# Another order for the end of a gated-attention MoE kernel: its flag is read earlier, its last branch is turned round and hinted at the head of the program

## The chip, the cores and the metric

The kernel runs on one core of a Trainium2 chip. A core has five engines that run their own instruction streams: PE (TensorE, matrix products), DVE (VectorE), ACT (ScalarE), POOL (GpSimd) and SP (SyncE, which here only starts DMA transfers). They meet at semaphores. What is measured is the device time of one launch in microseconds (us); the median of three runs of the kernel before is 1458.15 us (1458.13 to 1458.2).

## The reference

```python
def _attn_ref(q, k, v, f_logit):            # (4, 8, 768, 48) each
    f = 1.0 / (1.0 + np.exp(-f_logit))
    for t in range(S):
        state = f[:, :, t, :, None] * state + np.einsum('bhd,bhe->bhde', k[:, :, t], v[:, :, t])
        y[:, :, t] = np.einsum('bhd,bhde->bhe', q[:, :, t], state)

def _moe_ref(x, w_gate, w1, w2):            # x: (3072, 384), 8 experts, hidden width 1024
    P = np.exp(logits - logits.max())       # logits = x @ w_gate
    for _ in range(8):
        P /= P.sum(1, keepdims=True) + 1e-09
        P /= P.sum(0, keepdims=True) + 1e-09
        P *= N / E
    for e in range(E):
        out += P[:, e:e + 1] * (np.maximum(x @ w1[e], 0.0) @ w2[e])
```

The output of the attention, transposed, is the x of the MoE.

## The kernel before, in words

All products are made in half precision with every operand split into a high and a low part, three matmuls to a product. After the attention and the gate come the experts. Experts 0 and 1 are done early and densely. For experts 2 to 7 the work is cut into 48 periods (expert, half of the hidden width, batch), and each period has a first and a second half. The first half makes 15 products into PSUM banks named A to F and combines them (a scheme that saves products, after Strassen); a table of events (EVENTS, L69) says which engine adds, moves, converts what. It leaves tiles in SBUF: kh, kl, and the sums kr, kf with their high parts kgh (made on ACT, L1425) and low parts kgl (made on POOL, L1428). The second half is three blocks (`paired`, L1217; t = 0, 1, 2), seven products each into two PSUM tiles called kyps and kxps; ACT moves a partial sum back into PSUM (`move`, L1251), DVE adds the finished quarter into the accumulator acc (`add`, L1254), and for some blocks POOL adds a staged tile (L1301, L1275). In the last period of a batch the accumulator is stored to the output (`store`, L1266).

In the running part the blocks of one period are interleaved with the products of the next. At the end nothing is left to interleave, and a hand-written table, CLOSING (L87), says in which order the last events of period 47 and the five blocks that are left run. A number in it advances one of these blocks by one step (0 and 1 are blocks 1 and 2 of period 46; 2, 3 and 4 are blocks 0, 1 and 2 of period 47), a tuple is an event, and 'v' is a step of the computation of the flag. ENDX says which PSUM bank each of these blocks takes. `pin` and `mm` tie the instructions of each engine into the order in which the table writes them.

The flag: the kernel's gate uses a fast way that is right only for values within bounds; a test over the whole run ends as one integer, `flag`, made by five tiny DVE operations (tile gd_r, L919 to L924) and two transposes on PE. At the end each of the five engines loads it into a register (L271) and branches on it (L272): where it is set, `general`, a slow version of the whole computation, is run. The code of `general` stands right behind the fast path, the end of the program behind that, so in a normal run each engine jumps over `general`. At 'hint' in CLOSING a hint for that branch is given to DVE, ACT and SP; it names the block "general" as the likely target.

Of the kernel before, what the change touches and what calls it, by code (L numbers as in the profile page):

```python
# [8 lines left out]
F32 = mybir.dt.float32  # L9
# [73 lines left out]
READDAT = (9, 14)  # L83
CHECKAT = (1, 5)
MAXAT = (2, 6)
ENDX = (('x', None), ('k0', None), ('x', 'B'), ('k2', None))
CLOSING = (('add', 'C', '+', 3), ('gd', 1, 'P'), ('gh', 0, 1), 0, 1, 0, ('hh', 'D', 2), 0, ('gl', 0, 0), ('gl', 0, 1), 1,  # L87
# [5 lines left out]
BY_VECTOR = ((0, 0), (1, 0), (2, 0), (2, 1))  # L93
ORDER = [(e, m, b) for e in range(2, NE) for m in range(2) for b in range(B)]
PAIRED = (0, 1, 2)
BY_POOL = (1,)
# [169 lines left out]
def tile_gla_moe(tc, qkf, vc, vt, wg, w1, w2, out):  # L266
    nc = tc.nc
    with tc.tile_pool(name="fl", bufs=1) as fp:
        flag = fp.tile([1, 1], I32, name="flag")
        fast(tc, qkf, vc, wg, w1, w2, out, flag)  # L270
        bad = nc.values_load(flag, min_val=0, max_val=1)  # L271
        with tc.If(bad > 0, label="general"):  # L272
            general(tc, qkf, vt, wg, w1, w2, out)


# [1 line left out]
def fast(ctx, tc, qkf, vc, wg, w1, w2, out, flag):  # L277
# [615 lines left out]
    def verdict():  # L893
# [12 lines left out]
        pin(nc.vector.tensor_scalar(out=g[:, 0:2], in0=g[:, 0:2], scalar1=-1.0, scalar2=None, op0=ALU.mult))  # L906
        pin(nc.vector.tensor_scalar(out=g[:, 2:3], in0=g[:, 2:3], scalar1=-BALANCE, scalar2=None, op0=ALU.mult))
        yield
        ps = pk.tile([128, 128], F32, name="gd_t", tag="D")
        mm(transpose=True, out=ps[0:7, :], in_=g, identity=identf)  # L910
        yield
        col = cst.tile([7, 1], F32, name="gd_c")
        pin(nc.vector.tensor_reduce(out=col, in_=ps[0:7, :], axis=AX.X, op=ALU.max))
        yield
        ps = pk.tile([128, 128], F32, name="gd_s", tag="k1")
        mm(transpose=True, out=ps[0:1, 0:7], in_=col, identity=identf[0:7, 0:7])
        yield
        r = cst.tile([1, 9], F32, name="gd_r")
# [295 lines left out]
    first = {b: min(n for n, p in enumerate(ORDER) if p[2] == b) for b in range(B)}  # L1214
    final = {b: max(n for n, p in enumerate(ORDER) if p[2] == b) for b in range(B)}

    def paired(n, h, t, tag="x", own=None):  # L1217
        e, m, b = ORDER[n]
        new = n == first[b]
        if new and t == PAIRED[0]:  # L1220
            acc[b] = accp.tile([128, 2, TT, DM], F32, name=f"acc{b}", tag="acc")
        p = (pk if own else psm).tile([128, DM], F32, name=f"kyps_{n}_{t}", tag=own or "m")
        q = pk.tile([128, DM], F32, name=f"kxps_{n}_{t}", tag=tag)
        x0, y0, x1 = q[:, 0:DH], p[:, 0:DH], p[:, DH:DM]
        p2 = lp.tile([128, DH], F32, name=f"part_{n}_{t}", tag="part", bufs=2)
        by_pool = t in BY_POOL and n < len(ORDER) - 1 and not new
        xx, yy = (acc[b][:, v, t, :].rearrange("p (s d) -> p s d", s=2) for v in range(2))
        direct = n == len(ORDER) - 1
        if not new and not direct:
# [33 lines left out]

        def store(v, half):
            r0, ds = (2 * b + v) * HS + t * 128, slice(0, DM) if half is None else slice(half * DH, half * DH + DH)
            (nc.scalar if direct and v else nc.sync).dma_start(out=out[r0:r0 + 128, ds], in_=acc[b][:, v, t, ds])  # L1266

        product(y0, None, (0, 0), start=True)
        product(x1, (None, 0), (None, 0))
        yield  # L1270
        move(x0, y0)
        move(p2, x1, scale=scale(1))
        if direct:
            for i in range(2):
                pin(nc.gpsimd.tensor_tensor(out=yy[:, i, :], in0=yy[:, i, :], in1=p2, op=ALU.add))  # L1275
        yield
# [6 lines left out]
        yield  # L1283
        product(x1, (None, 1), (None, 1))
        yield
        out_x(0, x0)
        add(yy[:, 1, :], x1, scale(1), yy[:, 1, :] if direct else p2)
        halved = direct and t == PAIRED[-1]
        if halved:
            for v in range(2):  # L1290
                store(v, v)
        yield
# [5 lines left out]
        for v, z, there in ((0, xx, not by_pool), (1, yy, new or direct)):  # L1298
            if not there:
                y = acc[b][:, v, t, :]  # L1300
                pin(nc.gpsimd.tensor_tensor(out=y, in0=y, in1=z.rearrange("p s d -> p (s d)"), op=ALU.add))  # L1301
            if n == final[b]:
                store(v, 1 - v if halved else None)

    def readds():
        todo = {b: [(o, v, t) for t in range(TT) for v in range(2) for o in range(2) if (o, 2 * b + v) in RAW] for b in range(B)}
# [62 lines left out]
    def event(ctxt, ev):  # L1369
# [39 lines left out]
        elif kind == 'ga':  # L1409
            hs['a', ev[2]] = [lp.tile([128, 2, 128], F16, name=f"ka{q}_{tag}_{ev[2]}", tag=f"ka{q}{ev[2]}", bufs=1) for q in "hl"]  # L1410
            pin(nc.scalar.activation(out=hs['a', ev[2]][0], in_=bk[:, :, 0:128], func=AF.Relu))
        elif kind == 'gf':
            ah, al = hs['a', ev[2]]
            pin(nc.vector.scalar_tensor_tensor(out=al, in0=bk[:, :, 0:128], scalar=0.0, in1=ah, op0=ALU.max, op1=ALU.subtract))
        elif kind == 'gb':
            ah, al = hs['a', ev[1]]
            pin((nc.gpsimd if ev[2] == 'P' else nc.vector).tensor_tensor(out=al, in0=hs['r', ev[1]][:, 0], in1=ah, op=ALU.subtract))
        elif kind == 'gh':
            _, t, i = ev
            if not i:  # L1420
                if t == 2:
                    hs['g', t] = [[hp.tile([128, 2, 2, 128], F16, name=f"kg{q}{i}_{tag}_{t}", tag=f"k{q}1{0}{i}", bufs=1) for i in range(2)] for q in "hl"]
                else:
                    hs['g', t] = [[lp.tile([128, 2, 2, 128], F16, name=f"kg{q}{i}_{tag}_{t}", tag=f"kg{q}{t}{i}", bufs=1) for i in range(2)] for q in "hl"]
            pin(nc.scalar.activation(out=hs['g', t][0][i], in_=hs['f' if i else 'r', t], func=AF.Copy))  # L1425
        elif kind == 'gl':
            _, t, i = ev
            pin((nc.vector if tag == str(PERIODS - 1) and (t, i) in BY_VECTOR else nc.gpsimd).tensor_tensor(out=hs['g', t][1][i], in0=hs['f' if i else 'r', t], in1=hs['g', t][0][i], op=ALU.subtract))  # L1428
        elif kind == 'hh':
            pin(nc.scalar.activation(out=hs['h', ev[2]][0], in_=bk, func=AF.Relu))  # L1430
        else:
            hh, hl = hs['h', ev[2]]
            pin(nc.vector.scalar_tensor_tensor(out=hl, in0=bk, scalar=0.0, in1=hh, op0=ALU.max, op1=ALU.subtract))
# [56 lines left out]
        raise RuntimeError("an event was left")  # L1490

    def close(what):
        if what == 'v':
            next(judged, None)
        elif isinstance(what, tuple):
            event(ctxt, what)
        else:
            next(going[what], None)

    hint = CLOSING.index('hint')  # L1500
    for what in CLOSING[:hint]:
        close(what)
    with tc.block():
        tc.mark_branch_hint_location("general", "LikelyTaken", [mybir.EngineType.DVE, mybir.EngineType.Activation, mybir.EngineType.SP])
        for what in CLOSING[hint + 1:]:
            close(what)
    if any(next(block, going) is not going for block in going):
        raise RuntimeError("a block was left")
    for _ in judged:
# [2 lines left out]
        raise RuntimeError("an early output was not added")  # L1512
    for _ in chained((checks, maxima, judged)):
        raise RuntimeError("a check was left")


def _layout(q, k, v, f_logit, wg, w1, w2):
# [38 lines left out]
```

## Time and profile before

| what | value |
|---|---|
| median of three runs | 1458.15 us |
| the profiled execution's own time | 1458.26 us |
| its span, from the first to the last instruction | 1456.4 us |
| granted TensorE clock, mean | 0.999 of full speed |
| busy in the span: PE, DVE, ACT, POOL | 1438.7, 1232.9, 1061.1, 1045.1 us |

The span is what the trace covers; 1.86 us of the profiled execution lie around it. Times below are counted from the start of the span. PE's matmuls overlap, each row shows its start and its length, and the next starts before it ends. An engine's name with a q (SPq, PEldq) stands for its sequencer, which runs loads of registers, branches, waits on semaphores and starts of DMA transfers; these are not counted as busy.

### The profile page before, as it was taken

How to read it: one execution, taken by the hardware profiler on the slowest of the kernel's cores; microseconds unless marked ns; L12 is line 12 of the kernel's file. 1: busy time of each engine (PE TensorE's matmuls, PEld its weight loads, DVE VectorE, ACT ScalarE, POOL GpSimd, SP SyncE). 2: the span in 40 equal slices, each digit the busy share in tenths (PEclk: the TensorE clock that was granted, in tenths of full speed). 3: DMA queues.
4: the chain of work that ended last, by engine and by line, in shares of the span. 5: the costliest groups of instructions: out<-in, count | busy, mean ns of one | idle time of the engine just before them, and what ended most of it. 6: DMA issues, size and time to landing. Idle time of an engine off the chain costs nothing.

```text
span 1456.4 us, 40359 instructions
## 1 busy us (share of the span) xinstructions
PE 1438.7 (99%) x16054; PEld 1256.4 (86%) x16054; DVE 1232.9 (85%) x2512; ACT 1061.1 (73%) x2382; POOL 1045.1 (72%) x1227
## 2 busy tenths in 40 slices
PE   8999999999999999999999999999999999999997
PEld 5888876666666899999999999999999999999997
DVE  8888788885787899888899999888889888888876
ACT  7766666663354877888888888888877787778764
POOL 4344434446429576999999999999988888888764
PEclk9999999999999999999999999999999999999999
DMA  9455455541011101122212111111111110000012
GB/s 282 122 136 128 117 133 129 118 117 32 29 33 38 35 23 35 51 57 62 61 56 61 51 50 49 46 45 51 50 34 34 34 34 23 17 18 13 2 53 82
DMA packets 105271, 92.58 MB, mean 64 GB/s; under 512 B 72080, under 2 KB 91920, under 8 KB 105072
## 3 DMA queue, kind: packets, MB, share of 16 engines
q1 hardware_dynamic: 104496, 89.32, 22.7%
q8 instruction: 127, 2.08, 0.6%
q14 instruction: 72, 0.59, 0.1%
q10 hardware_dynamic: 576, 0.59, 0.1%
HBM read 64.03 MB, written 14.16 MB: 54 GB/s over the span
## 4 chain that ended last, share of the span: by engine, by line


## 5 line engine op out<-in xcount | busy, mean ns | idle before, releaser
L305 PEld LDWEIGHTS <-k1h 128*128 128x128 f16 x2880 | 270.9, 98 | 21.5 <-issue 2.9
L305 PE MATMUL kyps<-k2h,kgh 128*128 128x192 f16 x1152 | 283.4, 246 | 0.2 <-ACT part L1251 0.2
L305 PE MATMUL kyps<-k2l,kgh 128*128 128x192 f16 x1152 | 283.4, 246 | 0.0
L305 PE MATMUL kyps<-k2h,kgl 128*128 128x192 f16 x1152 | 283.4, 246 | 0.0
L305 PEld LDWEIGHTS <-kgh 128*128 128x128 f16 x2304 | 212.0, 98 | 6.7 <-issue 0.4
L1428 POOL TENSOR_TENSOR kgl<-kf,kgh 128x512 f16<-128x512 f32 x143 | 190.4, 1331 | 1.5 <-ACT kgh L1425 1.5
L1428 POOL TENSOR_TENSOR kgl<-kr,kgh 128x512 f16<-128x512 f32 x141 | 175.1, 1242 | 10.8 <-ACT kgh L1425 10.6
L1254 DVE SCALAR_TENSOR_TENSOR yy<-kyps,pes,part 128x192 f32<-128x192 f32 x258 | 106.7, 414 | 88.5 <-PE kyps L305 78.1
L1301 POOL TENSOR_TENSOR acc<-acc,yy 128x384 f32<-128x384 f32 x129 | 129.5, 1004 | 57.4 <-DVE yy L1254 57.4
L305 PEld LDWEIGHTS <-k1l 128*128 128x128 f16 x1440 | 140.9, 98 | 16.3
L305 PE MATMUL yps<-w2h,hl 128*128 128x384 f16 x384 | 125.1, 326 | 0.5 <-DVE hl L477 0.5
L305 PE MATMUL yps<-w2h,hh 128*128 128x384 f16 x384 | 125.1, 326 | 0.1
L305 PE MATMUL yps<-w2l,hh 128*128 128x384 f16 x384 | 125.1, 326 | 0.0
L305 PEld LDWEIGHTS <-w1h 128*128 128x128 f16 x1344 | 96.9, 98 | 32.0 <-ACT w1h L373 0.4
L305 PEld LDWEIGHTS <-kh 128*128 128x128 f16 x1152 | 108.2, 98 | 7.0 <-issue 0.6
L305 PEld LDWEIGHTS <-kgl 128*128 128x128 f16 x1152 | 112.7, 98 | 0.2 <-issue 0.2
L305 PEld LDWEIGHTS <-hh 128*128 128x128 f16 x768 | 73.6, 98 | 44.2 <-issue 0.5
L1251 ACT ACTIVATE kyps<-kyps 128x192 f32<-128x192 f32 x144 | 45.7, 317 | 80.0 <-PE kyps L305 78.5
L1425 ACT ACTIVATE kgh<-kf 128x512 f16<-128x512 f32 x144 | 91.8, 638 | 0.5 <-DVE kf L1402 0.5
L1425 ACT ACTIVATE kgh<-kr 128x512 f16<-128x512 f32 x144 | 91.6, 636 | 0.0
L1379 ACT ACTIVATE cp<-kb_A 128x512 f32<-128x512 f32 x144 | 86.3, 599 | 2.7 <-DVE kb_A L1381 2.0
L1405 POOL TENSOR_TENSOR kr<-kr 128x256 f32<-128x256 f32 x96 | 72.4, 754 | 17.3 <-PE kb_C L305 8.7
(306 smaller groups left out, 5248.0 us busy)
## 6 DMA issues: line engine op xcount, KB each, us to landing
q<-in_qkf_dram SPq DMA_DIRECT2D x23, 672.0 KB, 5.4
k1r<-in_w_dram SPq DMA_DIRECT2D x24, 384.0 KB, 3.1
ys<-yr SPq DMA_DIRECT2D x48, 192.0 KB, 2.1
k2r<-in_w_dram SPq DMA_DIRECT2D x24, 384.0 KB, 3.1
yb<-ys SPq DMA_DIRECT2D x48, 192.0 KB, 2.4
vr<-in_vc_dram SPq DMA_DIRECT2D x24, 192.0 KB, 4.9
out_dram<-acc SPq DMA_DIRECT2D x20, 192.0 KB, 1.9
w1r<-in_w_dram SPq DMA_DIRECT2D x8, 384.0 KB, 9.4
```

Source lines behind the costliest of these rows:

```text
L305: ins = (nc.tensor.transpose if transpose else nc.tensor.matmul)(**kw)
L1251: pin(nc.scalar.activation(out=out, in_=in_, func=AF.Copy, **kw))
L1254: pin(nc.vector.scalar_tensor_tensor(out=y, in0=ps, scalar=p, in1=z, op0=ALU.mult, op1=ALU.add))
L1301: pin(nc.gpsimd.tensor_tensor(out=y, in0=y, in1=z.rearrange("p s d -> p (s d)"), op=ALU.add))
L1379: pin(nc.scalar.activation(out=fresh(ev[2]), in_=bk, func=AF.Copy))
L1405: pin((nc.gpsimd if ev[2] == 'P' else nc.vector).tensor_tensor(out=r[:, 0], in0=r[:, 1], in1=r[:, 0], op=ALU.subtract))
L1425: pin(nc.scalar.activation(out=hs['g', t][0][i], in_=hs['f' if i else 'r', t], func=AF.Copy))
L1428: pin((nc.vector if tag == str(PERIODS - 1) and (t, i) in BY_VECTOR else nc.gpsimd).tensor_tensor(out=hs['g', t][1][i], in0=hs['f' if i el ...
```

## The change

The table CLOSING and the table of banks are written anew, with the flag's steps early and a new entry 'load'. There the load of the flag into a register is put on each engine, in the order of the table (on PE behind the last matmul). The low parts kgl of the last period, four of which were made on DVE (BY_VECTOR), are all made on POOL. Block 1 of period 46 has its x sums added by DVE and not by ACT and POOL. The last block has a PSUM tile of its own (kzps) for x1. In all 144 blocks the add that frees x1 is issued ahead of the one that reads x0. Every store of the last period is cut into two halves of 96 KB, eight on SP and four on ACT; before there were, for these, 192 KB stores and some halves. The branch now reads "where the flag is clear go to `settled`", which is the end of the program; `general` is the block it falls into otherwise. The hint names `settled` and is given to DVE, ACT and PE ahead of the first instruction of the fast path.

```diff
@@ -267,9 +266,11 @@
         flag = fp.tile([1, 1], I32, name="flag")
-        fast(tc, qkf, vc, wg, w1, w2, out, flag)
-        bad = nc.values_load(flag, min_val=0, max_val=1)
-        with tc.If(bad > 0, label="general"):
+        tc.mark_branch_hint_location("settled", "LikelyTaken", [mybir.EngineType.DVE, mybir.EngineType.Activation, mybir.EngineType.PE])
+        bad = fast(tc, qkf, vc, wg, w1, w2, out, flag)
+        with tc.If(bad < 1, label="settled", preferred_fallthrough_block=False) as settled:
+            pass
+        with settled.Else():
             general(tc, qkf, vt, wg, w1, w2, out)
@@ the tables (ENDX and CLOSING are rewritten; a line of each)
-ENDX = (('x', None), ('k0', None), ('x', 'B'), ('k2', None))
+ENDX = (('x',), ('k0', 'B'), ('x',), ('k2', None, 'D'))
-           4, 4, 3, 4, 4, 3, 4)
-BY_VECTOR = ((0, 0), (1, 0), (2, 0), (2, 1))
+           2, 1), ('hl', 'C', 1), ('gf', 'F', 2), 2, 2, 3, 1, 2, 2, 3, 3, 1, 3, 3, 2, 4, 4, 4, 'load', 2, 4, 4, 2, 3, 3, 3, 4, 4,
+           4, 4, 3, 3, 4, 4)
@@ the flag's two transposes
-        ps = pk.tile([128, 128], F32, name="gd_t", tag="D")
+        ps = pk.tile([128, 128], F32, name="gd_t", tag="B")
-        ps = pk.tile([128, 128], F32, name="gd_s", tag="k1")
+        ps = pk.tile([128, 128], F32, name="gd_s", tag="B")
@@ paired
-        x0, y0, x1 = q[:, 0:DH], p[:, 0:DH], p[:, DH:DM]
+        x0, y0 = q[:, 0:DH], p[:, 0:DH]
+        x1 = pk.tile([128, DH], F32, name=f"kzps_{n}_{t}", tag=other) if other else p[:, DH:DM]
-        by_pool = t in BY_POOL and n < len(ORDER) - 1 and not new
+        by_pool = t in BY_POOL and n < len(ORDER) - 2 and not new
-            (nc.scalar if direct and v else nc.sync).dma_start(out=out[r0:r0 + 128, ds], in_=acc[b][:, v, t, ds])
+            pin((nc.scalar if direct and t and half is not None and half != v else nc.sync).dma_start(out=out[r0:r0 + 128, ds], in_=acc[b][:, v, t, ds]))
         if direct:
+            yield
             for i in range(2):
+        add(yy[:, 1, :], x1, scale(1), yy[:, 1, :] if direct else p2)
         out_x(0, x0)
-        add(yy[:, 1, :], x1, scale(1), yy[:, 1, :] if direct else p2)
-        halved = direct and t == PAIRED[-1]
-        if halved:
+        if direct:
             for v in range(2):
                 store(v, v)
-                store(v, 1 - v if halved else None)
+                store(v, 1 - v if direct else None)
@@ the low parts
-            pin((nc.vector if tag == str(PERIODS - 1) and (t, i) in BY_VECTOR else nc.gpsimd).tensor_tensor(...))
+            pin(nc.gpsimd.tensor_tensor(...))
@@ the end
-    hint = CLOSING.index('hint')
-    for what in CLOSING[:hint]:
-        close(what)
-    with tc.block():
-        tc.mark_branch_hint_location("general", "LikelyTaken", [mybir.EngineType.DVE, mybir.EngineType.Activation, mybir.EngineType.SP])
-        for what in CLOSING[hint + 1:]:
-            close(what)
+    bad = []
+    for what in CLOSING:
+        close(what)
+    behind(held[0], order[-1])
...
+    return bad[0]
```

On SP, at the end of the fast path, acc3 is the accumulator of the last batch; 128x384 is a store of 192 KB, 128x192 one of 96 KB, and what an instruction waits for stands in brackets. Before:

```order
L1266 DMA out_0_dram<-acc3_9934 128x384 [waits DMAHW5_49,DVE_49]
L1503 UNCONDITIONAL_BRANCH
L1552 BRANCH_PREFETCH_HINT
L1266 DMA out_0_dram<-acc3_9934 128x192 [waits DMAHW6_49,DVE_49]
L1266 DMA out_0_dram<-acc3_9934 128x384 [waits DMAHW1_49,DVE_49]
L1266 DMA out_0_dram<-acc3_9934 128x192 [waits DMAHW3_49,DVE_49]
L1503 UNCONDITIONAL_BRANCH
L271 TENSOR_LOAD flag_58 [waits DVE_49]
L271 ISA x2
L272 COMPARE_AND_BRANCH
```

The same place on SP after the change:

```order
L1268 DMA out_0_dram<-acc3_9937 128x192 [waits DMAHW4_49,DVE_49]
L1268 DMA out_0_dram<-acc3_9937 128x192 [waits DMAHW5_49]
L1496 TENSOR_LOAD flag_58 [waits DVE_49]
L1496 ISA x2
L1268 DMA out_0_dram<-acc3_9937 128x192 [waits DMAHW6_49,DVE_49]
L1268 DMA out_0_dram<-acc3_9937 128x192 [waits DMAHW7_49]
L1268 DMA out_0_dram<-acc3_9937 128x192 [waits DMAHW0_49,DVE_49]
L1268 DMA out_0_dram<-acc3_9937 128x192 [waits DMAHW1_49]
L1268 DMA out_0_dram<-acc3_9937 128x192 [waits DMAHW2_49,DVE_49]
L1268 DMA out_0_dram<-acc3_9937 128x192 [waits DMAHW3_49]
L271 COMPARE_AND_BRANCH
```

SP had four stores of the last batch there and the load of the flag behind them; it now has eight, all halves, with the load ahead of six of them and the branch alone behind the last.

On ACT, in the last events and blocks (kgh is a high part, kyps and kxps are moves inside PSUM for the blocks of periods 46 and 47, part a scaled partial sum). Before:

```order
L1425 ACTIVATE kgh0_47_2_26474<-kr_47_2_26424 128x512 [waits DVE_49]
L1425 ACTIVATE kgh1_47_2_26475<-kf_47_2_26448 128x512 [waits DVE_49,PE_49]
L1251 ACTIVATE kxps_47_1_26485<-kyps_47_1_26484 128x192 [waits PE_49]
L1251 ACTIVATE part_47_1_26486<-kyps_47_1_26484,pes_114 128x192 [waits Pool_49]
L1266 DMA out_0_dram<-acc3_9934 128x384 [waits DMAHW4_49,DVE_49]
```

The same place on ACT after the change:

```order
L1427 ACTIVATE kgh0_47_2_26469<-kr_47_2_26356 128x512 [waits DVE_49,PE_49]
L1427 ACTIVATE kgh1_47_2_26470<-kf_47_2_26412 128x512 [waits DVE_49,PE_49]
L1253 ACTIVATE kyps_47_0_26416<-kyps_47_0_26416 128x192 [waits Activation_49]
L1253 ACTIVATE kxps_47_1_26455<-kyps_47_1_26454 128x192 [waits DVE_49]
L1253 ACTIVATE part_47_1_26456<-kyps_47_1_26454,pes_117 128x192 [waits Pool_49]
```

The move of block 0 of period 47 (kyps_47_0) stands behind the two high parts of block 2, which wait for PE; before, it came ahead of them, and the two were followed by the moves of block 1.

## Rows read from the trace of the kernel before

**Rows 1.** Busy time by engine in the running part: PE, PEld, DVE, ACT, POOL.

```profile
600.00:1430.00 830.00, 829.94 (x8864) 787.80 (x8863) 725.50 (x1529) 664.04 (x1529) 726.76 (x838) 1.00 0.14 41
```

**Rows 2.** Timeline of PE, 1435.5 to 1457: start, length, instruction, idle before.

```profile
1436.13 0.24 PE L305 MATMUL kyps<-k2h,kah 128*128 128x192 f16 x1 [0.99 <-ACT xx L1251]
1436.21 0.24 PE L305 MATMUL kyps<-k2l,kah 128*128 128x192 f16 x1
...
1438.01 0.24 PE L305 MATMUL kyps<-k2h,kgh 128*128 128x192 f16 x1 [0.23 <-ACT part L1251]
...
1442.09 0.24 PE L305 MATMUL kyps<-k2h,kh 128*128 128x192 f16 x1 [0.45 <-DVE acc L1254]
...
1449.24 0.25 PE L305 MATMUL kyps<-k2h,kgl 128*128 128x192 f16 x1
```

**Rows 3.** Timeline of DVE, its last two adds.

```profile
1449.53 0.74 DVE L1254 SCALAR_TENSOR_TENSOR acc<-kyps,pes,acc 128x192 f32<-128x192 f32 x2 [0.25 <-PE kyps L305]
```

**Rows 4.** The loads of the flag, line L271: ns min/median/max, first and last start.

```profile
L271 PEldq TENSOR_LOAD <-flag x1: 572/572/572, 1448.2 to 1448.2; - x1
L271 DVEq TENSOR_LOAD <-flag x1: 802/802/802, 1449.5 to 1449.5; - x1
L271 ACTq TENSOR_LOAD <-flag x1: 565/565/565, 1450.4 to 1450.4; - x1
L271 SPq TENSOR_LOAD <-flag x1: 568/568/568, 1450.7 to 1450.7; - x1
```

**Rows 5.** The branches and the first semaphores behind them, line L272.

```profile
L272 SPq EVENT_SEMAPHORE  x8: 17/17/17, 1454.5 to 1455.1; - x8
...
L272 PEldq COMPARE_BRANCH  x1: 4530/4530/4530, 1448.9 to 1448.9; - x1
...
L272 SPq COMPARE_BRANCH  x1: 78/78/78, 1451.6 to 1451.6; - x1
...
L272 DVEq EVENT_SEMAPHORE  x1: 21/21/21, 1453.8 to 1453.8; - x1
L272 ACTq EVENT_SEMAPHORE  x1: 17/17/17, 1454.0 to 1454.0; - x1
```

**Rows 6.** The end of the program and the hints, line L1552.

```profile
L1552 SPq EVENT_SEMAPHORE  x10: 17/28/28, 1455.1 to 1456.4; - x10
...
L1552 DVEq BRANCH_PREFETCH_HINT  x1: 51/51/51, 1443.3 to 1443.3; - x1
...
L1552 SPq BRANCH_PREFETCH_HINT  x1: 51/51/51, 1444.4 to 1444.4; - x1
```

**Rows 7.** DMA queues with any traffic, 1440.5 to 1448.9: packets, MB, share.

```profile
q1 hardware_dynamic: 535, 0.67, 21.5%
q10 hardware_dynamic: 144, 0.20, 6.4%
```

**Rows 8.** DMA issues, 1447 to 1448.5: KB each, us from issue to landing.

```profile
out_dram<-acc SPq DMA_DIRECT2D x1, 96.0 KB, 1.7
out_dram<-acc ACTq DMA_DIRECT2D x1, 96.0 KB, 2.4
```

**Rows 9.** The stores, line L1266, from 1448.5 on.

```profile
L1266 ACTq DMA_DIRECT2D out_dram<-acc x2: 338/338/338, 1449.0 to 1450.0; - x2
L1266 SPq DMA_DIRECT2D out_dram<-acc x2: 332/332/332, 1449.3 to 1450.3; - x2
...
DMA to landing us min/median/max: 3.9/4.1/4.5
```

**Rows 10.** The low parts made on DVE, line L1428, 1430 to 1457.

```profile
L1428 DVE TENSOR_TENSOR kgl<-kr,kgh x3: 733/831/1390, 1432.6 to 1442.0; 128x512 f16<-128x512 f32 x3
L1428 DVE TENSOR_TENSOR kgl<-kf,kgh x1: 678/678/678, 1443.9 to 1443.9; 128x512 f16<-128x512 f32 x1
```

**Rows 11.** The costliest groups of ACT on the page: busy us, mean ns.

```profile
L1251 ACT ACTIVATE kyps<-kyps 128x192 f32<-128x192 f32 x144 | 45.7, 317 | 80.0 <-PE kyps L305 78.5
L1425 ACT ACTIVATE kgh<-kf 128x512 f16<-128x512 f32 x144 | 91.8, 638 | 0.5 <-DVE kf L1402 0.5
```

More of the change, by code (lines that the diff above doesn't have):

```diff
@@ L85 @@
 MAXAT = (2, 6)
-ENDX = (('x', None), ('k0', None), ('x', 'B'), ('k2', None))
-CLOSING = (('add', 'C', '+', 3), ('gd', 1, 'P'), ('gh', 0, 1), 0, 1, 0, ('hh', 'D', 2), 0, ('gl', 0, 0), ('gl', 0, 1), 1,
[5 rows of a table removed]
-BY_VECTOR = ((0, 0), (1, 0), (2, 0), (2, 1))
+ENDX = (('x',), ('k0', 'B'), ('x',), ('k2', None, 'D'))
+CLOSING = (0, 'v', ('add', 'C', '+', 3), ('gd', 1, 'P'), ('gh', 0, 1), 1, ('hs', 'F', 2), 'v', 0, 'v', ('hh', 'D', 2), ('gl', 0,
[5 rows of a table added]
 ORDER = [(e, m, b) for e in range(2, NE) for m in range(2) for b in range(B)]
@@ L1215, in fast, with paired @@
     final = {b: max(n for n, p in enumerate(ORDER) if p[2] == b) for b in range(B)}
-    def paired(n, h, t, tag="x", own=None):
+    def paired(n, h, t, tag="x", own=None, other=None):
         e, m, b = ORDER[n]
@@ L1265, in store @@
             r0, ds = (2 * b + v) * HS + t * 128, slice(0, DM) if half is None else slice(half * DH, half * DH + DH)
-            (nc.scalar if direct and v else nc.sync).dma_start(out=out[r0:r0 + 128, ds], in_=acc[b][:, v, t, ds])
+            pin((nc.scalar if direct and t and half is not None and half != v else nc.sync).dma_start(out=out[r0:r0 + 128, ds], in_=acc[b][:, v, t, ds]))
         product(y0, None, (0, 0), start=True)
-        product(x1, (None, 0), (None, 0))
+        product(x1, (None, 0), (None, 0), start=other is not None)
         yield
@@ L1427, in event @@
             _, t, i = ev
-            pin((nc.vector if tag == str(PERIODS - 1) and (t, i) in BY_VECTOR else nc.gpsimd).tensor_tensor(out=hs['g', t][1][i], in0=hs['f' if i else 'r', t], in1=hs['g', t][0][i], op=ALU.subtract))
+            pin(nc.gpsimd.tensor_tensor(out=hs['g', t][1][i], in0=hs['f' if i else 'r', t], in1=hs['g', t][0][i], op=ALU.subtract))
         elif kind == 'hh':
@@ L1492, in close @@
     def close(what):
-        if what == 'v':
+        if what == 'load':
+            loads, (value,) = nc.values_load_multi_w_load_instructions(flag, min_val=0, max_val=1)
+            for ins in loads:
+                if ins.ins.engine != mybir.EngineType.PE:
+                    pin(ins)
+                else:
+                    held[0] = ins
+            bad.append(value)
+        elif what == 'v':
             next(judged, None)
```

7 rows, old and new, of the table CLOSING are left out of this document.

## The prediction

> **What bounds the kernel now.** First the table of busy time by stretches. In the running part, from 600 to 1430 us, PE is busy 829.94 of 830 us and DVE only 725.50 [rows 1], so up to there PE sets the pace, and nothing in the change takes an instruction from PE there. What can move the time is the tail. I read it engine by engine, PE's timeline first: the last matmul starts at 1449.24 and takes 0.25, so PE is through at 1449.5, and ahead of it PE stood idle three times, 0.99 for a move by ACT, 0.23 for ACT, and 0.45 for an add by DVE [rows 2]. Matmuls start 0.08 apart and last 0.24, so a restart loses the overlap of 0.16 too: 0.99 + 0.23 + 0.45 + 3 x 0.16 = 2.15 us lost. Then DVE's timeline: its last pair of adds starts at 1449.53, 0.74 for the two, 0.37 each [rows 3], so the numbers are complete in SBUF at 1450.27.
>
> The span ends at 1456.4, 6.1 us later, and this is the second place to look. The lines of the flag and the branch show what fills it. SP issues its last store at 1450.3 [rows 9], loads the flag from 1450.7 on, 0.57 [rows 4], branches at 1451.6, and its first instruction behind the branch comes at 1454.5 [rows 5], 2.8 us after the branch ended at 1451.7. From there it checks eight semaphores until 1455.1, ten more, and the last of the end's handshakes stands at 1456.4 [rows 6]: 1.9 us from the first semaphore, 1.3 from the eighth. Every branch has such a hole behind it. ACT: load ends at 1450.4 + 0.57 = 1451.0, next instruction 1454.0, 3.0 with the branch. DVE: 1449.5 + 0.80 = 1450.3 to 1453.8. PE's branch itself takes 4.53 us, from 1448.9 to 1453.4 [rows 4, 5]. The jump goes over the code of `general` to code that is not there yet: in 1440.5 to 1448.9, which begins before the three hints and covers them (1443.3 to 1444.4 [rows 6]), the only queues with traffic are the two that carry data, no queue of instructions among them [rows 7]. The hint before fetched nothing.
>
> A second limit lies right beside it. The stores issued from 1448.5 on land after 3.9 to 4.5 us, the last, issued at 1450.3, after about 3.9: 1454.2 [rows 9]. Two halves issued just before, between 1447 and 1448.5, took 1.7 and 2.4 [rows 8]. So late stores are slow in the same microseconds in which engines fetch code; if SP alone came through its branch at once, the landing at 1454.2 + 1.3 = 1455.5 would end the span only 0.9 earlier.
>
> **The change part by part.**
>
> *The tail's order on PE.* Gone: 2.15 us. New: ACT's move of block 0 of period 47 stands behind the two high parts of block 2, whose buffers PE must first release. When it does, ACT makes the second of them, 0.64, and then the move, 0.32 [rows 11], before PE can go on: 0.96 and a hand-over at each end, in all between 0.96 and the 0.99 + 0.16 + 0.08 = 1.23 of the largest hole before [rows 2]; I take 1.1. Two smaller waits on the way I put at the 0.23 of the small hole each, since the steps of the other blocks lie two products apart. That makes 1.1 + 0.46 = 1.6 and a gain of 0.55; at best, without the small ones, 1.05.
>
> *Low parts all on POOL.* DVE is rid of four conversions, 0.73, 0.83, 1.39 and 0.68 [rows 10], 3.6 us. It had no more to give PE than the 0.45 hole counted above. Of the same form the slowest took 1.39 and the one with POOL idle beside it 0.68: 0.71 more. POOL now has eight conversions nearly in a row and is never idle there, while DVE computes the flag. If two of the tiny operations on gd_r wait for POOL at 0.71 each, 1.4 of DVE's time goes, and what of it reaches PE would turn the gain to 0.55 - 1.4 = -0.85. The Trainium skill's "SBUF — State Buffer", section "SBUF: two separate sides", states that DVE with two SBUF inputs and GpSimd exclude each other for a whole instruction; the 1.39 beside 0.68 agrees. By that rule the waits are certain and the sum would lose up to 1.4. I take no loss for the sum, since DVE is rid of 3.6 us in the same stretch, and keep both ends: PE's end moves by +0.85 to -1.05; value 0.6 earlier.
>
> *The adds swapped in 144 blocks.* No instruction is added. What PE waits for is issued one add (0.37) earlier, what frees the other bank one later; with PE busy 829.94 of 830 there is nothing to gain. It could cost at most one add per block where the later bank is wanted at once, but the bank goes to a block several products on. I count nothing.
>
> *Stores.* On SP the eight halves cost eight issues of 0.33 [rows 9], 2.7 us, for four issues before, but the last two of SP's are the first halves of block 2, finished four adds before DVE's end: 1450.27 - 0.6 - 4 x 0.37 = 1448.2. Their two issues end at 1448.9. The four on ACT come last: the last pair waits for DVE's end at 1449.67, so the last issue starts at 1449.67 + 0.34 = 1450.0 against 1450.3 before.
>
> *The flag earlier.* SP's load, 0.57 [rows 4], its checks and their gaps, about 1.3 between the last store's issue and the branch, leave the place behind the last store and go into the queue ahead of six stores. What is queued behind that load waits 0.9, but those stores wait for DVE anyway. So SP branches at about 1449.0 (0.3 either way) in place of 1451.6. That is the largest sure gain on SP's side: 2.6.
>
> *The branch and the hint.* SP has no hint in either form that worked, so it pays 0.08 + 2.8: first semaphore at 1449.0 + 2.9 = 1451.9, end at 1453.8. The two removed jumps per engine at L1503 and the hint itself (0.05 [rows 6]) are nothing. For PE, ACT and DVE nothing in the trace shows a hint at the head, 1450 us ahead of its branch. Its bounds: it works, and the branch costs under 0.1; or it does nothing, and each pays 3.0 (PE 4.5) again. I take it that it works, since now the named block is the one that is jumped to; only by a little.
>
> *The sum, if it works.* Stores with few fetches beside them land in 1.7 to 2.4 [rows 8]: 1450.0 + 2.4 = 1452.4, plus 1.3 = 1453.7. SP's own way: 1453.8. They nearly agree; the later gives a span of 1453.8 in place of 1456.4. With the 1.86 us around it, 1455.7; the profiled execution (1458.26) lies 0.11 over the median of 1458.15, so 1455.6.
>
> **Rivals.**
>
> *A, the forecast: the hint works on three engines and SP's unhinted branch is what is left.* For it: the hint before named the block that followed anyway, so its failing says little. Against: nothing of it is seen. 1455.6; with PE's end and SP's queue at their bounds, 1454.8 to 1456.6.
>
> *B, the hint has no effect.* For it: three hints before left no fetch [rows 6, 7]; and between the hint at the head and the branch lie all of PE's matmuls, 8864 in the running part alone [rows 1]. Then ACT branches at 1450.0 + 0.34 + 0.1 = 1450.4 and comes through at 1453.4, its end no later than SP's with its chain of semaphores; but PE, DVE and ACT fetch while the last stores are under way, so these land after 3.9 to 4.1 as before: 1450.0 + 4.0 + 1.3 = 1455.3. With 1.86 less 0.11: 1457.1, and if the fetches are spread more, with a landing of 3.3, 1456.4. I name 1456.9. The Trainium skill's "Runtime: NRT & Kernel Launch", section "Instruction fetch mechanics", says that prefetch is purely sequential through two pages and that a taken branch out of them must fetch its target first. By that rule no hint of so long ago could hold its page, and B would be certain; the holes of 2.8 and 4.53 us agree with it, but no run here shows a hint that names the right block.
>
> *C, slower: the hint is acted on too early.* The engine fetches the end's page in place of the next page in line, once or more, and stands still until the right one is there. The price by PE's row is 4.53 us each [rows 5]; A's gain is 2.55, so the first such stall on PE after its start decides: 1455.6 + 4.5 = 1460.1, and a second makes it 1464.6. Against it: a hint that broke the straight way would be of no use anywhere.
>
> *D, DVE's waits on POOL.* Priced above: PE ends 0.85 later than before; in A the last landing then comes 1.45 later, and 0.1 of slack against SP's way is left of it: 1455.6 + 1.35 = 1457.0. This is inside the range.
>
> **How the numbers follow.** A 0.53, B 0.33, D 0.07, C 0.07. A measurement of this kernel can tell about 0.2% from no change, 2.9 us: faster means under 1455.2, slower over 1461.1. A reaches under 1455.2 in less than half of its cases (it takes a PE end at its best, or landings of 1.7), say 0.24 in all. Slower by over 0.2% takes two stalls of C or a cost that I don't see: 0.05. The rest, 0.71, is within 0.2%. The range: A's lower bound 1454.8 less 0.3 for a landing at 1.7, 1454.5; upwards B whole, 1457.1, and 0.4 for a later PE: 1457.5. C lies outside.
>
> **What would show it.** In the changed profile: PE's last matmul at about 1448.9 and holes of 1.5 us in place of 2.15, the largest of them behind ACT; DVE's operations on gd_r, two of them long if D holds; SP's branch near 1449.0 with 2.8 to its first semaphore; PE's branch at 0.1 and not 4.5 if the hint works, ACT's and DVE's next instruction within 0.2; the last stores landing after about 2.4. The forecast is wrong if PE's branch still takes 4.5 (B), if PE shows holes of over 2 us in its running part (C), or if SP reaches its branch after 1450.

## The result, and the profile after

The changed kernel takes 1472.13 us (median of 6, 1472.03 to 1473.02), the kernel before on the same chip 1458.14 (6 runs, 1457.88 to 1458.2): ratio 1.0097, interval 1.0084 to 1.011. It is 14.0 us slower, where 2.5 us less were forecast. The profiled run's span is 1470.4 us for 1456.4 before.

The loss lies in the running part. Busy time by stretches, the kernel before (PE, PEld, DVE, ACT, POOL, in brackets the number of instructions; then the granted clock, the share of DMA and GB/s):

```profile
520.00:1120.00 600.00, 599.94 (x6411) 569.57 (x6408) 539.20 (x1133) 490.42 (x1127) 538.90 (x635) 1.00 0.17 49
1120.00:1400.00 280.00, 280.00 (x2992) 265.81 (x2991) 239.72 (x510) 216.03 (x499) 228.79 (x258) 1.00 0.07 22
```

The same two stretches after:

```profile
520.00:1120.00 600.00, 593.83 (x6260) 555.51 (x6258) 547.96 (x1104) 482.79 (x1100) 524.38 (x615) 1.00 0.17 48
1120.00:1400.00 280.00, 279.90 (x2990) 265.64 (x2988) 239.07 (x504) 217.34 (x500) 233.49 (x268) 1.00 0.08 23
```

In the same 600 us PE gets through 151 matmuls fewer; at 600 / 6411 = 0.094 us each that is 14.1 us, the whole difference. From 1120 us on it loses nothing, though the adds are swapped there too. Between 520 and 1120 us DVE has fewer instructions and yet 8.8 us more of busy time. Which of them grew is shown by the groups of DVE (busy us, mean ns), before:

```profile
L1110 DVE SCALAR_TENSOR_TENSOR k1l<-k1r,k1h 128x256 f16<-128x256 f32 (+1 forms) x48 | 34.0, 709 | 0.0
L1135 DVE SCALAR_TENSOR_TENSOR k2l<-k2r,k2h 128x192 f16<-128x192 f32 (+1 forms) x48 | 28.9, 603 | 0.0
L1135 DVE SCALAR_TENSOR_TENSOR k2l<-k2s,k2h 128x768 f16<-128x768 f32 x24 | 25.3, 1054 | 0.0
```

and after, the same operations (one line further down in the code):

```profile
L1111 DVE SCALAR_TENSOR_TENSOR k1l<-k1r,k1h 128x256 f16<-128x256 f32 (+1 forms) x48 | 39.8, 830 | 0.0
L1136 DVE SCALAR_TENSOR_TENSOR k2l<-k2r,k2h 128x192 f16<-128x192 f32 (+1 forms) x48 | 38.2, 797 | 0.0
L1136 DVE SCALAR_TENSOR_TENSOR k2l<-k2s,k2h 128x768 f16<-128x768 f32 x24 | 33.9, 1411 | 0.0
```

These are the low parts of the weights; each reads two tiles from SBUF. They take 5.8 + 9.3 + 8.6 = 23.7 us more for the same work. With the fourth such group, k1l<-k1s, they took 113.2 us after and 89.7 before in the stretch from 520 to 1120 us; from 1120 to 1400 us, where nothing is lost, 39.5 and 38.7. One place shows how. DVE before:

```profile
535.54 0.40 DVE L1260 TENSOR_SCALAR acc<-kxps,pes 128x192 f32<-128x192 f32 x1
536.15 0.42 DVE L1254 SCALAR_TENSOR_TENSOR acc<-kyps,pes,part 128x192 f32<-128x192 f32 x1 [0.20 <-PE kyps L305]
536.48 0.44 DVE L1110 SCALAR_TENSOR_TENSOR k1l<-k1r,k1h 128x256 f16<-128x256 f32 x1
```

POOL before, beside it:

```profile
536.60 1.33 POOL L1428 TENSOR_TENSOR kgl<-kr,kgh 128x512 f16<-128x512 f32 x1
```

DVE after (the times of after are 0.11 ahead here):

```profile
536.04 0.42 DVE L1256 SCALAR_TENSOR_TENSOR acc<-kyps,pes,part 128x192 f32<-128x192 f32 x1 [0.52 <-PE kyps L306]
536.37 0.41 DVE L1262 TENSOR_SCALAR acc<-kxps,pes 128x192 f32<-128x192 f32 x1
536.70 1.24 DVE L1111 SCALAR_TENSOR_TENSOR k1l<-k1r,k1h 128x256 f16<-128x256 f32 x1
```

POOL after:

```profile
536.50 1.16 POOL L1430 TENSOR_TENSOR kgl<-kr,kgh 128x512 f16<-128x512 f32 x1
```

Before, DVE made the x0 add while PE was still at x1's product; then came x1's add, and the conversion began 0.12 ahead of POOL's operation, so it was POOL that waited (1.33 in place of 1.16). After, x1's add stands in front, DVE waits 0.52 for it with the x0 add behind it, and the conversion begins 0.20 behind POOL's operation: it takes 1.24 in place of 0.44 and ends 0.28 behind POOL's end.

From there the delay reaches PE. DVE's next read of the bank kb_D, before:

```profile
537.56 0.70 DVE L1384 TENSOR_TENSOR kb_F<-kb_D,cp 128x512 f32<-128x512 f32 x1
```

and after, with PE's matmuls beside it:

```profile
538.58 0.70 DVE L1386 TENSOR_TENSOR kb_F<-kb_D,cp 128x512 f32<-128x512 f32 x1
...
538.96 0.25 PE L306 MATMUL kyps<-k2h,kgl 128*128 128x192 f16 x1
539.33 0.27 PE L306 MATMUL kb_D<-xah,k1h 128*128 128x256 f16 x1
```

DVE is through with the bank at 539.28, and PE's next product into it starts at 539.33, 0.37 behind the matmul ahead of it and not 0.08. Between 520 and 1120 us PE stops in this way 45 times, 13.4 us in all: 22 times ahead of a product into kb_D, 12 times into kb_A, 11 times into kb_B, all banks of a first half. It never stops there ahead of a product into kyps or kxps, the tiles that the two swapped adds read and free. Before, none of these stops is there.

The tail, which the forecast was about, moved little. PE's waits from 1434 us on, after, in us in all, times and longest [rows 2 are those of before]:

```profile
PE kyps L306 <- DVE yy L1256: 1.1, 1, 1.1
PE kyps L306 <- ACT kyps L1253: 0.9, 1, 0.9
PE kyps L306 <- DVE acc L1256: 0.6, 1, 0.6
```

Its last matmul, after:

```profile
1464.16 0.25 PE L306 MATMUL kzps<-k2h,kgl 128*128 128x192 f16 x1
```

That is 14.92 later than before. With 14.1 of it lost between 520 and 1120 us, the tail itself is 0.8 to 0.9 us slower and not 0.6 faster. The prediction's way of adding up the holes says the same: the three waits stand idle for 1.06, 0.85 and 0.64 us, with 3 x 0.16 for the restarts 3.03 lost for 2.15 before. The branches, after [rows 5]:

```profile
L271 SPq EVENT_SEMAPHORE  x8: 17/17/17, 1468.2 to 1469.0; - x8
...
L271 PEldq COMPARE_BRANCH  x1: 419/419/419, 1463.8 to 1463.8; - x1
L271 PEldq EVENT_SEMAPHORE  x1: 51/51/51, 1464.5 to 1464.5; - x1
...
L271 SPq COMPARE_BRANCH  x1: 58/58/58, 1465.2 to 1465.2; - x1
L271 ACTq COMPARE_BRANCH  x1: 68/68/68, 1467.5 to 1467.5; - x1
L271 ACTq EVENT_SEMAPHORE  x1: 17/17/17, 1468.0 to 1468.0; - x1
```

and the stores, after, from 1455 us on [rows 9]:

```profile
L1268 ACTq DMA_DIRECT2D out_dram<-acc x4: 384/442/1843, 1464.2 to 1467.1; - x4
```

PE's branch takes 0.42 in place of 4.53, ACT is through 0.5 after its branch in place of 3.0; SP, without a hint, needs 2.9. But one of ACT's stores stood 1.84 us at its issue. From the last matmul's start to the end of the span there are now 6.2 us and before 7.2. So 14.1 + 0.9 - 1.0 = 14.0, as measured.

### The profile page after: what moved, and what is told of

Same layout as the page of the kernel before. It is cut to its first block, busy times and chain, and to the rows that moved or that the text cites. A ratio compares the mean times of both kernels' runs of the same rounds, so it can differ in the third digit from the quotient of the medians.

```text
span 1470.4 us, 40390 instructions
## 1 busy us (share of the span) xinstructions
PE 1447.7 (98%) x16054; PEld 1256.0 (85%) x16054; DVE 1252.6 (85%) x2510; ACT 1064.8 (72%) x2380; POOL 1046.8 (71%) x1230
## 4 chain that ended last, share of the span: by engine, by line
PE 85%; DVE 9%; ACT 3%; issue 2%; POOL 1%; DVEq 0%; ACTq 0%; POOLq 0%
PE kyps L306 24%; PE yps L306 14%; PE hps L306 12%; PE kb_A L306 8%; PE kb_B L306 7%; PE kb_D L306 6%; PE kxps L306 4%; PE kb_C L306 4%; PE kb_E L306 2%; PE kb_F L306 2%; DVE k1l L1111 1%; PE aps L306 1%; DVE yy L1256 1%; PE kvps L306 1%; POOL kgl L1430 1%
## 5 line engine op out<-in xcount | busy, mean ns | idle before, releaser
L1430 POOL TENSOR_TENSOR kgl<-kf,kgh 128x512 f16<-128x512 f32 x144 | 196.6, 1365 | 5.0 <-ACT kgh L1427 5.0
L1430 POOL TENSOR_TENSOR kgl<-kr,kgh 128x512 f16<-128x512 f32 x144 | 167.9, 1166 | 10.8 <-ACT kgh L1427 10.8
L1407 POOL TENSOR_TENSOR kr<-kr 128x256 f32<-128x256 f32 x96 | 75.7, 789 | 17.2 <-PE kb_C L306 8.7
```

What stands on the lines that cost most here:

```text
L1430: pin(nc.gpsimd.tensor_tensor(out=hs['g', t][1][i], in0=hs['f' if i else 'r', t], in1=hs['g', t][0][i], op=ALU.subtract))
```

## The experiments

**What the running part lost.** The rival to the swap was the hint at the head or the new layout of the code. First the changed kernel with the old order in all blocks up to period 45:

```diff
+        if n < len(ORDER) - 2:
+            out_x(0, x0)
         add(yy[:, 1, :], x1, scale(1), yy[:, 1, :] if direct else p2)
-        out_x(0, x0)
+        if n >= len(ORDER) - 2:
+            out_x(0, x0)
```

> The changed kernel with the two adds in the old order (x0 first, then x1) in all blocks up to period 45; tail, flag, stores, branch and hint as changed. Theory 1 (the swap costs it: the x0 add now waits behind an add whose product PE makes one product later, DVE comes late to the weight conversions, and these then wait out POOL): the 14.0 us that PE lost between 520 and 1120 us come back, about 1458.1 us (1457.6 to 1458.6), and no drift of PE before 1430 us. Rival theory 2 (the hint at the head, or the code's new layout, slows the running part): still 1472.

Measured 1458.58 us (11 runs), ratio to before 1.0004 (0.9995 to 1.0013). Then the swap alone, in the kernel before:

```diff
-        out_x(0, x0)
         add(yy[:, 1, :], x1, scale(1), yy[:, 1, :] if direct else p2)
+        out_x(0, x0)
```

> The kernel before with nothing changed but the order of the two adds, in all 144 blocks. Theory 1: 1458.1 + 14.0 = 1472.1 us (1471 to 1473), lost between 520 and 1120 us. Theory 2: 1458.1.

Measured 1471.31 us, ratio 1.009 (1.0076 to 1.0103). The two lines carry 13.2 of the 14.0 us. With them back in the old order 0.4 is left over the kernel before, which the interval does not tell from nothing; hint, tail and layout together carry no more than that.

**Why two lines cost that.** Is it the wait for x1, or that x1's add comes first? An operation that only reads an element of x1 makes DVE wait without swapping anything:

```diff
+        if not direct:
+            pin(nc.vector.tensor_scalar(out=peek, in0=x1[0:1, 0:1], scalar1=1.0, scalar2=None, op0=ALU.mult))
         out_x(0, x0)
         add(yy[:, 1, :], x1, ...)
```

> The kernel before, adds in its own order, with one added DVE operation ahead of the pair in every block but the last period's: it copies a single element of x1 out of PSUM (its result is not used). So the x0 add waits for x1's product as in the swapped order, but x1's add is not ahead of it. Theory 1a (what costs is that DVE stands waiting for x1 and loses the time in which it would have done the x0 add): about as slow as the swap, 1469 to 1474 us, with the loss between 520 and 1120 us. Rival 1b (the swap costs because x1's add is done earlier or x0's bank comes free later): within 2 us of e6_peek_x0.

The control:

```diff
-            pin(nc.vector.tensor_scalar(out=peek, in0=x1[0:1, 0:1], ...))
+            pin(nc.vector.tensor_scalar(out=peek, in0=x0[0:1, 0:1], ...))
```

> The same with the added operation reading an element of x0, on which the next add waits anyway: the control for the cost of the operation itself (141 times some 0.1 us of DVE). Theory 1a: 1458 to 1463 us, well under e5_peek_x1. Rival 1b: the same as e5_peek_x1 within 2 us.

Measured 1471.39 (ratio 1.0089, 1.0073 to 1.0104) against 1458.66 (1.0003, 0.9993 to 1.0012). Standing still for x1 is enough; that x1's add comes first is not needed. The bank of x0 comes free later in e5_peek_x1 too, so the two runs alone do not rule out the second half of rival 1b. PE's stops do: in e5_peek_x1 they are again at kb_D, kb_A and kb_B (43 times, 12.7 us) and never at a tile of the adds. The last run here leaves the swap in and takes work from POOL: its adds of the early experts' sums do 8 of 384 columns, so most of these sums is missing from the output.

```diff
-                    pin(nc.gpsimd.tensor_tensor(out=y, in0=y, in1=yt, op=ALU.add))
+                    pin(nc.gpsimd.tensor_tensor(out=y[:, 0:8], in0=y[:, 0:8], in1=yt[:, 0:8], op=ALU.add))
```

> As e2_swap_only, but POOL's 48 adds that bring in the early experts' sums do 8 of 384 columns each, so most of the sums of experts 0 and 1 is left out of the output and POOL has about 45 us less to do between 520 and 1120 us. Theory 1c (DVE's lost 0.3 us per block grows to PE's 14 us only because DVE's weight conversions then meet POOL at work): conversions near their lengths of before, 3 us or less lost, 1458 to 1461 us. Rival 1d (standing still before x1 alone eats up DVE's slack): still 1468 or more.

Measured 1463.07 us, ratio 1.0033 (1.002 to 1.0047): between the two. Its 520 to 1120 us:

```profile
520.00:1120.00 600.00, 597.69 (x6352) 564.40 (x6350) 542.71 (x1122) 488.40 (x1117) 495.05 (x626) 1.00 0.17 49
```

59 matmuls short of before, 5.5 us. Over all four conversion groups the time above before's 141.3 us was 23.9 us after, 22.4 with the swap alone, 19.5 with the peek at x1, 8.3 here and -2.9 with the peek at x0, and PE lost 14.1, 13.2, 13.3, 5.5 and 0.5. So it is for the larger part the meeting with POOL that turns the wait into lost time, and neither expectation had the size. What stays is in one group, k2l<-k2r, with 38.7 us as with the swap alone (38.2; 28.9 before); the other groups are back near their times of before. No run takes the work from POOL without the swap, so how much shorter the conversions would be there is open.

**The tail.** In the tail of the change three operations on gd_r, of one element each, take long:

```profile
L921 DVE TENSOR_TENSOR gd_r<-gd_r x1: 917/917/917, 1447.7 to 1447.7; 1x1 f32<-1x1 f32 x1
L922 DVE SCALAR_TENSOR_TENSOR gd_r<-gd_r x1: 1112/1112/1112, 1448.6 to 1448.6; 1x1 f32<-1x1 f32 x1
L924 DVE SCALAR_TENSOR_TENSOR gd_r<-gd_r x1: 1007/1007/1007, 1451.4 to 1451.4; 1x1 f32<-1x1 f32 x1
```

Before going at them, the hint: without it, and then with it on all five engines, both on e1_no_swap.

```diff
-        tc.mark_branch_hint_location("settled", "LikelyTaken", [mybir.EngineType.DVE, mybir.EngineType.Activation, mybir.EngineType.PE])
```

> As e1_no_swap, without the hint at the head. If the hint is what made the branches of PE, DVE and ACT short in the changed kernel, PE's branch takes about 4.5 us again and ACT and DVE need about 2.9 from branch to next instruction; ACT then comes through at about 1456.4 and the time is 0.7 to 1.4 us over e1_no_swap. If the turned branch alone does it, the branches stay short and the time is that of e1_no_swap within 0.2.

Measured 1459.94 (1.0004 to 1.0022 of before), 1.4 over e1_no_swap, though the intervals overlap, and both kernels have runs that are some 2 us longer than their others (see the last section), so the price of the hint cannot be read from these two times. The branches decide:

```profile
L270 PEldq COMPARE_BRANCH  x1: 3873/3873/3873, 1449.8 to 1449.8; - x1
...
L270 ACTq COMPARE_BRANCH  x1: 54/54/54, 1452.9 to 1452.9; - x1
...
L270 ACTq EVENT_SEMAPHORE  x1: 17/17/17, 1456.0 to 1456.0; - x1
```

The hint makes the branches short, not the turned condition.

```diff
-        ...mybir.EngineType.PE])
+        ...mybir.EngineType.PE, mybir.EngineType.SP, mybir.EngineType.Pool])
```

> As e1_no_swap, with SP and POOL named in the hint too. SP's first semaphore comes about 0.5 us after its branch and not 2.9. If the last landing of the stores sets the end (in the changed kernel the eighth semaphore stood 0.02 us behind it), the time is that of e1_no_swap within 0.3 us; if SP's missing code sets it, it is 0.8 to 2.4 us less.

Measured 1458.47 (0.9993 to 1.0011), 0.1 under e1_no_swap: SP's first semaphore came 0.5 behind its branch, but its eighth at 1455.2, with the last landing. The landing sets the end. With this kernel as the base, the three operations read one operand from PSUM:

```diff
-        ...tensor_tensor(out=r[:, 7:8], in0=r[:, 4:5], in1=r[:, 6:7], op=ALU.mult)
+        ...tensor_tensor(out=r[:, 7:8], in0=ps[0:1, 4:5], in1=r[:, 6:7], op=ALU.mult)
```

(and likewise in0 of the second and in1 of the third).

> As e4_hint_all, with the three operations on gd_r (L921, L922, L924) reading one of their operands from PSUM, so that none reads two vectors from SBUF. Theory 4 (in the new tail these three wait out POOL for 0.91, 1.11 and 1.01 us, and DVE's lateness is what PE waits for): each takes about 0.2, PE's holes in the tail shrink from 2.9 to about 1.3 us, PE ends 1 to 1.5 us earlier, and the time is 0.7 to 1.5 under e4_hint_all. Rival (the waits of the tail come from PE's own order and ACT): the three become short and the time stays within 0.3.

Measured 1457.55 (0.9985 to 1.0003), 0.9 under e4_hint_all, as expected; PE's last matmul starts at 1449.65 for 1450.38. PE's holes shrank by less than expected. From one matmul's start to the next they were 0.9 and 1.3 us behind DVE and 1.1 behind ACT; the one of 1.3 is gone, the one of 0.9 is now 1.2, and the one behind ACT is as it was. The operations:

```profile
L921 DVE TENSOR_TENSOR gd_r<-gd_s,gd_r x1: 145/145/145, 1434.0 to 1434.0; 1x1 f32<-1x1 f32 x1
L922 DVE SCALAR_TENSOR_TENSOR gd_r<-gd_s,gd_r x1: 206/206/206, 1434.2 to 1434.2; 1x1 f32<-1x1 f32 x1
L924 DVE SCALAR_TENSOR_TENSOR gd_r<-gd_r,gd_s x1: 133/133/133, 1436.1 to 1436.1; 1x1 f32<-1x1 f32 x1
```

**The branch alone**, in the kernel before: turned, hinted at the head for five engines, or for three as in the change, nothing else.

```diff
+        tc.mark_branch_hint_location("settled", "LikelyTaken", [DVE, Activation, PE, SP, Pool])
         fast(tc, qkf, vc, wg, w1, w2, out, flag)
         bad = nc.values_load(flag, min_val=0, max_val=1)
-        with tc.If(bad > 0, label="general"):
+        with tc.If(bad < 1, label="settled", preferred_fallthrough_block=False) as settled:
+            pass
+        with settled.Else():
             general(tc, qkf, vt, wg, w1, w2, out)
...
-    with tc.block():
-        tc.mark_branch_hint_location("general", ...)
```

> The kernel before with its own tail, its own stores and the flag loaded at the end, with only the branch turned round and the hint at the head, for all five engines. No engine has a hole of 2.6 to 4.5 us behind its branch. Theory 3 (the fetches of the five engines delay the last stores): SP's first semaphore at 1452.2, the last store, issued at 1450.3, lands after 2.4 in place of 3.9; the end at 1454.2, 1456.0 us in all, 2 less than before. Rival (landings as slow as before): 1457.2.

> As e7_branch_all, with the hint for PE, DVE and ACT only, as in the change. SP pays its 2.8 us again: branch at about 1451.1, first semaphore at 1453.9, end at 1455.9. If the landing of the last stores sets the end in e7_branch_all (1454.6 there, and the eighth semaphore cannot pass it), the time is that of e7_branch_all within 0.3 us; if SP's hole sets it, 0.5 us or more over it.

Measured 1457.75 (0.9987 to 1.0006) and 1457.81 (0.9989 to 1.0007). The gain is 0.4 and 0.3, which the intervals do not tell from nothing, and not 2, and SP's hint is worth nothing: the last store lands at 1454.6 and 1454.1, as late as before (1454.2). POOL, hinted in e7_branch_all, still has 2.3 us behind its branch there, for 0.6 in e4_hint_all; it is through at 1451.0, ahead of the last landings, and why it is slow there was not followed up.

**What makes the last stores late.** First, fewer stores on ACT:

```diff
-            pin((nc.scalar if direct and t and half is not None and half != v else nc.sync).dma_start(...))
+            pin((nc.scalar if direct and t and half is not None and half != v and v else nc.sync).dma_start(...))
```

> As e9_psum_flag, with two of ACT's four stores moved to SP, so that ACT issues two and SP ten. Theory 5 (ACT's third store in a row waits 1.2 to 1.9 us at issue, and so its fourth lands last): no issue on ACT over 0.6 us, ACT's branch 1.8 us earlier, the last landing at about 1453.9 in place of 1454.4, the time 0.3 to 0.6 us less. Rival (the queue of SP now has the same stall, or a ring held by a fetch of code lands last anyway): within 0.2 us of e9_psum_flag.

Measured 1457.72 (0.9987 to 1.0005): no gain, and the stall went along to SP:

```profile
L1268 SPq DMA_DIRECT2D out_dram<-acc x7: 384/424/2193, 1448.0 to 1452.7; - x7
```

So it is not ACT's queue. In both versions a fetch of 16 KB of code on queue q8 begins 0.8 to 0.9 us behind the end of PE's branch, at 1450.5 and 1450.6, and takes 1.6 to 1.7. The issue that stands still ends 0.39 behind the end of that fetch in both, and 0.37 and 0.39 behind it in the changed kernel and in e4_hint_all. PE can be made to branch later:

```diff
+    ps = pk.tile([128, 128], F32, name="late", tag="B")
+    mm(transpose=True, out=ps[0:1, :], in_=acc[B - 1][:, 0, TT - 1, DH:DH + 1], identity=identf)
     behind(held[0], order[-1])
```

> As e9_psum_flag, with one tiny transpose on PE behind the last matmul that reads the column DVE writes last, so that PE loads the flag and branches about 1 us later; its result is not used. Theory 6 (the fetch of 16 KB on queue q8, some 0.8 us behind PE's branch and 1.6 long, holds one of the 16 DMA engines while the last stores pass; an issue stalls 1.8 to 2.2 us on it, be it on ACT or SP, and the last landing is that engine's): the fetch starts at about 1452 in place of 1450.5, no issue on ACT is over 0.7 us, the last landing comes at about 1452.7 in place of 1454.4, the time is 1 to 1.7 us under e9_psum_flag, about 1456.2, and faster than both kernels. Rival (stalls and late landings come from the number of stores in flight): within 0.3 us of e9_psum_flag.

Measured 1458.01 (0.999 to 1.0009): the stall is gone, five of the last six stores land by 1453.1, but the sixth meets the fetch, now at 1452.2, and lands at 1454.9. The trace has sixteen completions for a store; fifteen of this one's came by 1453.3, and only the last at 1454.9. The expected time was missed, and one more step was needed, eight matmuls of 512 columns behind that transpose:

```diff
+    ps = pk.tile([128, 512], F32, name="later", tag="B")
+    for i in range(8):
+        mm(out=ps, lhsT=ind[:, 0:128], rhs=ind[:, 0:512], start=True, stop=True)
     behind(held[0], order[-1])
```

> As e12_late_pe, with eight more matmuls of 512 columns on PE ahead of its load of the flag (their result is not used), 0.21 us each: PE branches 1.7 us later than in e12_late_pe, at about 1452.7, and its fetch of 16 KB starts at about 1453.9. Theory 6: that is behind the stores' last data, so the last store, issued at 1451.0, lands after 1.9 to 2.4 and not after 3.9, at about 1453.2 in place of 1454.9; PE's own first instruction behind the branch comes at 1453.2; the end at 1454.6, 1456.3 us in all, 1.7 under e12_late_pe and 1.8 under the kernel before. Rival (the last of many stores lands late whatever PE fetches): 1458.0 as in e12_late_pe.

Measured 1456.50 us (11 runs, 1456.37 to 1457.65) against 1457.99 (15 runs, 1457.71 to 1458.58): ratio 0.9991, interval 0.9982 to 1.0000. The interval just reaches 1, but every run of it is shorter than every run of the kernel before. It is the fastest version here, 1.5 us under the kernel before, and 15.6 under the change. PE's load ran beside the matmuls, so its branch came 0.5 later than in e12_late_pe and not 1.7. Its first instruction behind the branch came 1.0 later, at 1452.5, and the fetch at 1453.2; that was enough, and the last store landed at 1453.4 for 1454.9. Stores from 1445 us on, e9_psum_flag:

```profile
L1268 ACTq DMA_DIRECT2D out_dram<-acc x4: 385/448/1772, 1449.7 to 1452.5; - x4
...
DMA to landing us min/median/max: 1.6/1.9/3.8
```

and e13_later_pe:

```profile
L1268 ACTq DMA_DIRECT2D out_dram<-acc x4: 385/432/461, 1449.6 to 1451.0; - x4
...
DMA to landing us min/median/max: 1.6/1.8/2.7
```

## Why the prediction was wrong, point by point

- *The adds swapped in 144 blocks: "I count nothing".* This step failed: 13.2 us by e2_swap_only, 14.1 in the stretch from 520 to 1120 us of the changed kernel. It asked only who waits for the two banks, and not when the inputs of the two adds are ready: x0's product ends one product ahead of x1's, so the x0 add had been done in a gap that the swap closes. About the banks it was right, PE never stops at them; the cost came by another way, from DVE's conversions, which started later and met POOL, to the banks of the first half. And from PE's 829.94 of 830 us [rows 1] it read that there is nothing to gain and looked no further, when DVE, 725.50 of 830 there, was the engine to look at; in 520 to 1120 us it was at 539.20 of 600. e1_no_swap, e2_swap_only, e5_peek_x1 and e6_peek_x0 show it from both sides. Without the swap the forecast would still have been too low, by the steps below: e1_no_swap took 1458.58, and its upper bound was 1457.5.
- *Two vectors from SBUF beside POOL.* The rule of the Trainium skill's "SBUF — State Buffer", section "SBUF: two separate sides", an exclusive hold of the shared ports for a whole instruction, was used for the tiny operations alone and not for the 168 conversions of the running part, where the same 0.71 of [rows 10] applied. The runs agree with it: 1.24 beside POOL for 0.44 ahead of it, and 0.91, 1.11 and 1.01 for operations of one element that take 0.13 to 0.21 with a PSUM operand.
- *The tail's order on PE: 0.6 earlier.* Wrong by 1.5. The hole through ACT's move is there, 0.85 idle, 1.0 with the restart, as worked out. The other two are not 0.23 but 0.64 and 1.06, both behind DVE: rival D, to which 0.07 was given, and whose price of 1.4 was for two waits where there are three, 2.5 of excess. e9_psum_flag took the excess away; one of the two holes behind DVE went with it, the other stayed, and 0.9 came back.
- *The hint: it works on three engines.* Right: 0.42 for 3.87 us on PE, 0.4 for 3.0 on ACT (against e3_no_hint). The rule of the Trainium skill's "Runtime: NRT & Kernel Launch", section "Instruction fetch mechanics", that a jump out of the pages that were fetched in line must first fetch its target, agrees with SP's 2.9 without a hint; by it alone B would have come, and the hinted engines decide against that. Of the hint before, [rows 7] show no fetch between 1440.5 and 1448.9; one of 16 KB had begun at 1440.45, but that is ahead of the three hints, so the reading stands.
- *SP branches 2.6 earlier.* It branched 0.78 us behind PE's end for 2.1 before: 1.4 earlier against PE, since its last pair of stores was released only at 1463.9, 1.0 ahead of DVE's end and not four adds of 0.37, and the two issues of that pair took 1.2 and not 0.66.
- *Stores with few fetches land in 2.4.* Failed: 3.6 to 4.1 for five of the last six. The fetch that PE's jump itself sets off is not saved by the hint; stall and late landing come and go with it (e10_act_two, e12_late_pe, e13_later_pe). That it holds one of the 16 DMA engines is the reading that was tested; which engine carries which transfer the trace does not show, only that in the late store of e12_late_pe one of sixteen completions was late. That is why a working hint gained 0.4 at most and not 2.
- *Rival C*, the only one on the slower side, named a mechanism that does not show here: in e1_no_swap PE loses nothing before 1430 us.

## What to carry to other kernels

An engine runs in order: before two of its operations change places, ask for each when its input is ready, not only who waits for its result. Of an engine that is nearly full, ask which operations behind it get longer when they start 0.3 us later, above all those that share a port with another busy engine. And a code fetch behind a jump is a transfer like any other; put it where no store waits.

## What was not expected of the hardware

A one-element DVE operation took 1.11 us beside POOL, and 0.21 with one operand in PSUM. A DMA issue on ACT or SP took 1.8 to 2.2 us while 16 KB of code were fetched, and at most 0.48 in e12_late_pe and e13_later_pe, where the fetch came later. The fetch alone does not do it: in the kernel before, the issues at 1450.0 and 1450.3 [rows 9] lay inside a fetch of 16 KB, from 1449.8 to 1451.7, and took 0.34 and 0.33, with fewer stores under way. How many it takes was not tested. And in 4 of 11 runs e1_no_swap took 1459.9 to 1460.3 where the others took 1457.8 to 1458.8; in the profiled one of these, after holes of 0.9, 1.3 and 1.1 us in PE's work, the clock granted was 0.53, the lower level of 1.2 GHz, nearly all through 3.5 us:

```profile
1435.00:1443.00 8.00, 5.49 (x63) 5.04 (x61) 7.87 (x18) 3.75 (x10) 5.47 (x7) 1.00 0.14 52
1443.00:1446.50 3.50, 3.46 (x23) 3.27 (x23) 0.74 (x2) 0.86 (x3) 3.05 (x4) 0.53 0.16 59
1446.50:1452.00 5.50, 5.50 (x68) 5.49 (x67) 2.89 (x9) 1.05 (x3) 1.14 (x2) 0.99 0.43 146
```

With the same holes e4_hint_all kept 1.00 there. What decides between the two was not settled.
